# A planner's constants and twelve halved warm-up products in a two-layer attention kernel

## The chip, the core and the metric

The kernel runs on one core of a Trainium2 chip. The metric is the device time of one execution in microseconds; runs of the same kernel are given by their median and their spread. The profile is of one execution, and its times run from the first instruction.

## The reference, cut to what matters

```python
a = softmax over s of phi                      # 4 batches, 8 heads, 576 rows, 32 memory slots
k_m, v_m = a^T k, a^T v                        # 32 x 64 for each head
attn = softmax(q k_m^T / 8)                    # over the 32 slots
x = (attn @ v_m) as 2304 x 512
g = max(0.01 h, h), h = x @ w_in;   x = g @ w_out        # d_ff = 2048
g = h * tanh(softplus(h)), h = x @ w_in2; out = g @ w_out2
```

q, k, v and phi are float32; the four weight matrices arrive as float64, so the kernel has to turn each 64-bit number into a float32 by itself.

## The kernel before, in words

**Work on TensorE (PE).** Products that need float32 accuracy are made from halves: each operand is split into a rounded part (hi) and a remainder (lo), and three products hi*hi, lo*hi, hi*lo are summed. In the first layer the value matrix is folded into the weight: `vw` = v_m times a 512-wide chunk of w_in (L975), and then an item (batch, half of 288 rows, block m of 128 hidden units) is 6 products `h_t <- at_t, vw_t` (L1226) and, two items later, 12 products `acc_t <- hi_t or lo_t, wo_t` (L1259). There are 128 items. The turns are: batch 0 chunk 0 (items 0 to 7), batch 0 chunk 1 (8 to 15), batch 1 chunks 0 and 1 (from item 16), and so on. The second layer (L1579, L1791) begins near 375 us.

**The start.** Before item 0 the kernel needs batch 0's attention (phi softmax, its products L508, norm and transposes L819, q transposes L865, scores L892, softmax, then `at_t` hi and lo) and the first chunk of w_in. While PE has nothing to do it runs warm-up products: `FILL=58` products identity times identity, 128 x 128 in float32 (L1057, `spin`). They are a chain of tasks of priority 4.9, their result is not used, and the planner puts one wherever PE is idle in its plan. A float32 product of this kind stands in the trace as two records, and each record has a weight load of its own.

**Weights from float64.** `decode` takes a raw block of 128 x 512 numbers in two 32-bit words: ScalarE (ACT) scales the high word (L369), the low word is shifted right by 29 (`top`: on ACT at L374 or on VectorE, DVE, at L376), and DVE joins the two (L411). For w_out a block then gets a rounded copy (L310 on ACT or L312 on DVE) and a remainder (L326 on DVE); this is `wo_unit`. The raw blocks go round a ring of three buffers `raw` and four `raws`, in the order of the program: eight blocks of chunk 0 (four of w_in, then w_out 0 to 3), then four of w_in's chunk 1, then w_out 4 to 7.

**The order.** The program's order on every engine, and the order of the loads on the one DMA queue (SP), comes from a planner that runs while the kernel is built (`Order.run`): at each moment of its own modelled time it starts the ready task of the smallest priority number on the engine that would end it first (estimated cost plus a bias). A task that takes a buffer waits until the buffer is free. The result is fixed: each engine then runs its list in order on the chip. The constants in `K` set priorities in units of items:

- `WO`: w_out block m has the priority m - WO. `WC`: w_in's chunk c has that of its first item less WC; `V0` is the same for its product L975.
- `A1`: batch 1's attention starts that many items before item 16; `PL` and `QL` set how much earlier its loads come. `BH`: a load of batch 1 may not be issued before a certain load of w_in's chunk 1 (entry 9 means none).
- `V2`: the same as V0 for batches 2 and 3. `HFD`: the step of priority between the parts of batch 0's softmax.
- `TOP`: the bias in us against DVE when the planner chooses where `top` runs; ACT is planned at 0.61 us and DVE at 0.60 us plus `TOP`.

The planner takes a warm-up product as 0.44 us for the first 20 and 0.22 us after that, whatever its shape.

Of the kernel before, what the change touches and what calls it, by code (L numbers as in the profile page):

```python
# [23 lines left out]
def hop(a, b):  # L24
# [4 lines left out]


K = dict(
    LAG1=2, WIN=8, OB=2, RS=4, FILL=58, A1=10, S1=8.0,
    A2=30, S2=2.6, V1=2.4, V2=14, W2=45, W2S=3.8, O='phi0 kv0 phi1 q0 w0 kv1 q1 w1 w2 w3', HF0=-20.0, HF1=-7.0,
    HFD=0.3, TOP=0.1, HI=0.2, WO=2.0, WOL=1, WC=3.0, WC0=-38.0, V0=3.0, COLD=20, GL=1.5, AL=5.0, XL=22.0, T='0:1 0:1 1:2 0:2 1:2', SB=1,
    DW=280e3, DQ=1.3, DP=1.2, DS=0.78, DI=0.38, L4=0.5, L4P=1.6, L4S=0.8, L4T=5.0, MA=6, QL=4, PL=6, BH=(9,3,3,3,3), FK=-52.5, DWF=0.85, MV="......rvvrrvvrvr",
)


# [121 lines left out]
def kernel(  # L160
# [12 lines left out]
    nc = tc.nc  # L173
# [4 lines left out]
    P = 128  # L178
# [14 lines left out]
    RQ = S // 32  # L193
    LAG1 = K['LAG1']

# [75 lines left out]
    ident = const.tile([P, P], F32, name="ident")  # L271
# [11 lines left out]
    def add(engines, prio, fn, deps=(), take=(), use=(), bias=None):  # L283
        t = sched.add(engines, prio, fn, deps, take, use, bias)
        for b in (*take, *use):
            if b.pool is spool:
                early.append(t)
            elif b.pool is rawpool:
                middle.append(t)
        return t  # L290


    def dve(n):
        return n / 960 + 0.065
# [4 lines left out]
    def act(n, ps=False):  # L299
        return n / 1196 + (0.051 if ps else 0.093)  # L300

    def mm(n, count=1):
        return count * (n / 2400 + 0.0133)

    def mb(shape_bytes):
        return shape_bytes / K["DW"]

# [531 lines left out]
    def score_tasks(b, g, pq, ps, dp):  # L839
        sp = b < K['SB'] and g == 1  # L840
        if sp:
            qT, qb = qT_s.new([P, HG, NB1]), q_s.new([P, RQ, D])
            qT_v, qb_v = (lambda: qT.t), (lambda: qb.t)
        else:
            qT = qb = kvq.new([P, 2, RQ * D])
            qT_v = lambda: qb.t[:, 1].rearrange("p (h c) -> p h c", h=HG)
            qb_v = lambda: qb.t[:, 0].rearrange("p (r d) -> p r d", r=RQ)
        parts, firsts_q = [], []
        q_g = q[b, g * HG:(g + 1) * HG]

        def ld(e):
            qb.make()
            dma(out=qb_v(), in_=q_g.rearrange("h (p r) d -> (h p) r d", r=RQ))

        lq = add({"SP": K["DS"] * mb(589824)}, PQ[g], ld, (), [qb])
        for i in range(3):
            ps_b = h_tag.new([P, 3, P])

            def ftr(e, ps_b=ps_b, i=i):
                ps_b.make()  # L860
                if sp and not i:
                    qT.make()
                for j in range(3):
                    r = 2 * (3 * i + j)
                    nc.tensor.transpose(ps_b.t[:, j], qb_v()[:, r:r + 2, :].rearrange("p r d -> p (r d)"), ident)  # L865

            tt = add({"PE": 0.34}, pq + 0.7 * i, ftr, [lq, *firsts_q[:1]], [ps_b, qT] if sp and not i else [ps_b], [qb])

            firsts_q.append(tt)

            def fcp(e, i=i, ps_b=ps_b):
                copy(e, qT_v().rearrange("p h (c j) -> p j h c", j=9)[:, 3 * i:3 * i + 3], ps_b.t.rearrange("p j (h c) -> p j h c", h=HG))

            parts.append(add({"ACT": act(840, True), "DVE": dve(840)}, pq + 0.7 * i + 0.2, fcp, [tt], (), [ps_b, qT]))
        a = at_tag.new([P, 2, S], F32R)
        ab = []
        for hf in range(2):
            half(b, g, hf, ps[hf], dp, qT, qT_v, parts, a, ab)
        at[b, g] = (a, ab[0:2], ab[2:4])
# [173 lines left out]

    warm = acc_tag.slots[3].new([P, P])

    def spin(e):
        nc.tensor.matmul(out=warm.t if hasattr(warm, "t") else warm.make(), lhsT=ident, rhs=ident, start=True, stop=True)  # L1057

    last = None
    for i in range(K["FILL"]):  # L1060
        last = add({"PE": 0.44 if i < K["COLD"] else 0.22}, 4.9, spin, [last], [] if i else [warm], [warm] if i else [])
    for g in range(NG):
        kv_norm(0, g, -60.0 + 10 * g, 1.0, *kv_first(g, -60.0 + 10 * g, 1.0))
    for g in range(NG):
        score_tasks(0, g, -59.5 + 10 * g, (-54.0, K["HF0"]) if not g else (-40.0, K["HF1"]), K["HFD"])
    def next_batch(b):
        d, st = (K["A1"], K["S1"]) if b == 1 else (K["A2"], K["S2"])
        p = base[b] - d
        kv_rest(b, p, 0.08 * d / 2)
        score_rest(b, p + 0.1 * d, (p + 0.3 * d, p + 0.3 * d + st), 0.03 * d)  # L1070
# [42 lines left out]
    for n in range(NM):  # L1113
# [57 lines left out]
        def save2(e, u=u, wd=wd):  # L1171
# [13 lines left out]
                out=sb.t.rearrange("p a f -> p (a f)").bitcast(F32R), in0=sb.t.rearrange("p a f -> p (a f)"),  # L1185
# [26 lines left out]
    def passes(n):  # L1212
        return [(j, wi) for j in range(n) for wi in range(2)]

    def stage1(i, b, sub, m):
# [41 lines left out]
        def mms(todo):  # L1257
            for kk, wi, src in todo:
                nc.tensor.matmul(  # L1259
                    out=ac[kk].t,  # L1260
                    lhsT=wu[0].t[:, wi, kk * P:(kk + 1) * P],
                    rhs=(hb if src == 0 else lb).t,
                    start=(first and (wi, src) == (0, 0)),
                    stop=(last and src == 1),
                )

        hs = []
        if first:
            for kk in range(NK):
# [3 lines left out]

                hs.append(add({"PE": mm(NB1, 2)}, i + LAG1 + 0.01 * kk, f, [t4, *wu[1:], *hs[-1:]], [ac[kk]], [hb, wu[0]]))
        else:
            hs.append(
                add(
                    {"PE": mm(NB1, 2 * NK)}, i + LAG1, lambda e: mms([(kk, wi, 0) for kk, wi in passes(NK)]),
                    [t4, *wu[1:], *prev_l], (), [hb, wu[0], *ac.values()],
# [3 lines left out]
        if last:  # L1283
            for kk in range(NK):
                tl = add(
                    {"PE": mm(NB1)}, i + LAG1 + 0.1 + 0.01 * kk, lambda e, kk=kk: mms([(kk, 0, 1)]),
                    [t5, *hs], (), [lb, wu[0], ac[kk]],
# [21 lines left out]
                if add_in:  # L1309
                    deps.append(evs[kk, sub])  # L1310
                evs[kk, sub] = add(
                    {"DVE": dve(NB1)} if add_in else {"ACT": act(NB1, True), "DVE": dve(NB1)},
                    i + LAG1 + 0.2, fe, deps, [xb] if fresh else [], [ac[kk]] if fresh else [ac[kk], xb],
                )
        else:
            tl = add(
                {"PE": mm(NB1, NK)}, i + LAG1 + 0.1, lambda e: mms([(kk, 0, 1) for kk in range(NK)]),
                [t5, *hs], (), [lb, wu[0], *ac.values()],
# [577 lines left out]
```

## Time and profile before

| what | value |
|---|---|
| median of 3 runs | 742.42 us (742.01 to 742.64) |
| the profiled execution | 741.87 us |
| its span, first to last instruction | 740.1 us |
| PE busy | 731.0 us (99%) |
| DVE, ACT busy | 550.6 us (74%), 402.5 us (54%) |
| share of PE in the chain that ended last | 96% |

Some 1.8 us of the execution lie outside the span. Busy time of PE is the union of its records, whose ends are modelled; a wait shorter than that modelled tail does not show as idle time, so starts of successive records are compared as well.

### The profile page before, as it was taken

To read this page: it belongs to the slowest core of one execution; us is meant where nothing else is said; L and a number is where in the kernel's file an instruction comes from. 1 tells how busy PE (TensorE), PEld (TensorE's weight loads), DVE (VectorE), ACT (ScalarE), POOL (GpSimd) and SP (SyncE) were. 2 spreads that over 40 slices of the span, in tenths; PEclk is the share of its full clock that TensorE was granted. 3 is DMA by queue.
4 is the path that set the end of the run, shared out by engine and by line. 5 is a ranking of instruction groups with operands and counts; after the bars stand their busy time and mean duration, and the time that the engine had idled before them with its cause. 6 is when DMAs were issued, how large, how long until landed. Compare 5 with 4: busy or idle time off the path is not lost.

```text
span 740.1 us, 15587 instructions
## 1 busy us (share of the span) xinstructions
PE 731.0 (99%) x5875; PEld 701.3 (95%) x5875; DVE 550.6 (74%) x1153; ACT 402.5 (54%) x877; POOL 0.7 (0%) x6
## 2 busy tenths in 40 slices
PE   8999999999999999999999999999999999999997
PEld 7788899888999989999999999999999999999997
DVE  6899868598766965647859797867777966775595
ACT  4866458565553775645546665544464644444442
POOL 0000000000000000000000000000000000000000
PEclk9999999999999999999999999999999999999999
DMA  9793957787869587863559898788988778996475
GB/s 353 299 318 115 350 172 232 229 274 229 290 207 286 171 274 269 262 233 101 199 199 338 302 312 254 233 271 249 300 278 264 250 239 258 297 290 207 126 218 182
DMA packets 99322, 183.73 MB, mean 248 GB/s; under 512 B 8112, under 2 KB 51376, under 8 KB 99248
## 3 DMA queue, kind: packets, MB, share of 16 engines
q1 hardware_dynamic: 99248, 182.75, 75.5%
q8 instruction: 46, 0.75, 0.4%
q14 instruction: 28, 0.23, 0.1%
HBM read 140.25 MB, written 42.47 MB: 247 GB/s over the span
## 4 chain that ended last, share of the span: by engine, by line
PE 96%; DVE 2%; ACT 1%; DMA 0%; issue 0%
PE acc_t L1259 28%; PE h_t L1579 22%; PE acc_t L1791 22%; PE h_t L1226 13%; PE misc_t L1791 2%; PE misc_t L975 2%; PE acc_t L1579 2%; PE acc_t L508 1%; PE misc_t L741 1%; PE misc_t L646 1%; DMA phi_t<-in_phi_dram 0%; PE h_t L865 0%; ACT raws_t L369 0%; ACT raws_t L374 0%; PE misc_t L689 0%
## 5 line engine op out<-in xcount | busy, mean ns | idle before, releaser
L1259 PE MATMUL acc_t<-hi_t,wo_t 128*128 128x288 f32 x1024 | 160.6, 297 | 0.4 <-DVE x_t L312 0.3
L1259 PEld LDWEIGHTS acc_t<-hi_t,wo_t 128*128 128x128 f32 x1024 | 142.9, 188 | 12.2 <-issue 7.0
L1226 PE MATMUL h_t<-at_t,vw_t 128*128 128x288 f32 x768 | 123.1, 296 | 0.0
L1791 PE MATMUL acc_t<-hi_t,wo_t 128*128 128x384 f32 x448 | 114.4, 336 | 0.0
L1240 ACT ACTIVATE hi_t<-h_t 128x288 fp32r<-128x288 f32 x128 | 52.6, 411 | 111.8 <-PE acc_t L1259 105.3
L1226 PEld LDWEIGHTS h_t<-at_t,vw_t 128*128 128x128 f32 x768 | 108.5, 188 | 0.7 <-issue 0.6
L1247 DVE TENSOR_TENSOR lo_t<-e_t,hi_t 128x288 fp32r<-128x288 f32 x128 | 57.3, 450 | 47.4 <-ACT e_t L1240 21.6
L1259 PE MATMUL acc_t<-lo_t,wo_t 128*128 128x288 f32 x512 | 89.8, 297 | 0.5 <-DVE lo_t L1247 0.5
L1791 PEld LDWEIGHTS acc_t<-hi_t,wo_t 128*128 128x128 f32 x448 | 81.3, 188 | 0.0
L1259 PEld LDWEIGHTS acc_t<-lo_t,wo_t 128*128 128x128 f32 x512 | 74.7, 188 | 6.3 <-issue 5.6
L1579 PE MATMUL h_t<-xt_t,vw_t 128*128 128x384 f32 x396 | 79.4, 336 | 0.0
L1579 PE MATMUL h_t<-xt_t,wo_t 128*128 128x384 f32 x352 | 75.8, 336 | 0.0
L1791 PE MATMUL acc_t<-lo_t,wo_t 128*128 128x384 f32 x224 | 75.6, 337 | 0.0
L1758 DVE TENSOR_TENSOR lo_t<-wo_t,hi_t 128x384 fp32r<-128x384 f32 x94 | 52.0, 554 | 31.4 <-ACT hi_t L310 29.9
L1579 PEld LDWEIGHTS h_t<-xt_t,vw_t 128*128 128x128 f32 x396 | 69.3, 188 | 0.0
L310 ACT ACTIVATE hi_t<-wo_t 128x384 fp32r<-128x384 f32 x78 | 40.7, 524 | 40.7 <-PE acc_t L1791 36.4
L1579 PEld LDWEIGHTS h_t<-xt_t,wo_t 128*128 128x128 f32 x352 | 61.9, 188 | 0.0
L1240 ACT ACTIVATE e_t<-h_t 128x288 f32<-128x288 f32 x128 | 52.0, 406 | 0.0
L1791 PE MATMUL acc_t<-wo_t,hi_t 128*128 128x256 f32 x240 | 45.0, 282 | 0.0
L1604 ACT ACTIVATE wo_t<-wo_t 128x384 f32<-128x384 f32 x53 | 27.6, 522 | 30.8 <-DVE wo_t L1598 30.6
L1791 PEld LDWEIGHTS acc_t<-lo_t,wo_t 128*128 128x128 f32 x224 | 42.0, 188 | 0.0
L310 ACT ACTIVATE wo_t<-h_t 128x384 f32<-128x384 f32 x50 | 24.5, 489 | 31.1 <-PE h_t L1579 31.1
(263 smaller groups left out, 1110.0 us busy)
## 6 DMA issues: line engine op xcount, KB each, us to landing
wo_t<-tscr SPq DMA_DIRECT2D x168, 256.0 KB, 3.8
vw_t<-wsum SPq DMA_DIRECT2D x32, 512.0 KB, 4.7
win_t<-wscr SPq DMA_DIRECT2D x24, 512.0 KB, 5.5
raw_t<-in_moe_w_in_dram SPq DMA_DIRECT2D x19, 512.0 KB, 7.5
raw_t<-in_moe_w_out_dram SPq DMA_DIRECT2D x17, 512.0 KB, 5.5
wsum<-vw_t SPq DMA_DIRECT2D x16, 512.0 KB, 4.5
wo_t<-wsum SPq DMA_DIRECT2D x16, 512.0 KB, 4.3
tscr<-raw_t SPq DMA_DIRECT2D x9, 512.0 KB, 5.5
```

The source lines that it names most:

```text
L310: nc.scalar.activation(out=o, in_=i, func=AF.Copy)
L508: nc.tensor.matmul(out=acc.t[rows, :].rearrange("p (j d) -> p j d", j=2), lhsT=phv()[rows, r, :], rhs=kv.t[rows, :2304].rearrange("p (j r ...
L646: nc.tensor.matmul(out=accs_[g].t[o:o + M, :].rearrange("p (j d) -> p j d", j=2), lhsT=ph.t[rows, x, j, :], rhs=kv[g].t[rows, :, x % 2, j, :],
L975: nc.tensor.matmul(out=pss[g].t[M * (h ^ g):M * (h ^ g) + M, :], lhsT=vT[b, g][0].t[rows, g, h ^ g if b else h // 2, :], rhs=wbs[g].t[rows ...
L1226: nc.tensor.matmul(out=h.t, lhsT=us[g][0].t[:, wi, j0:j0 + P], rhs=ats[g][0].t[:, ai, cols], start=(n == 0), stop=(n == 3 * NG - 1),)
L1240: nc.scalar.activation(out=o, in_=h.t, func=AF.Prelu, alpha=0.01)
L1247: lambda e: nc.vector.tensor_tensor(out=lb.make(), in0=eb.t, in1=hb.t.bitcast(F32), op=ALU.subtract),
L1259: nc.tensor.matmul(out=ac[kk].t, lhsT=wu[0].t[:, wi, kk * P:(kk + 1) * P], rhs=(hb if src == 0 else lb).t, start=(first and (wi, src) == ( ...
L1579: nc.tensor.matmul(out=h.t, lhsT=w[:, wi, c0:c0 + P], rhs=xp[b, xi].ap()[:, j], start=(first and j == 0 and k3 == 0), stop=(j == 1 and k3 ...
L1604: lambda e: nc.scalar.activation(out=t_of[x](), in_=h.t if h else t_of[x](), func=AF.Mish),
L1758: lambda e, hb=hb, lb=lb, src=src: nc.vector.tensor_tensor(out=lb.make(), in0=src(), in1=hb.t.bitcast(F32), op=ALU.subtract),
L1791: nc.tensor.matmul(out=ac[t].t, lhsT=T[:, wi, t * P:(t + 1) * P] if wide else x.t[:, t * P:(t + 1) * P], rhs=x.t if wide else T[:, wi], st ...
```

## The change

It sets ten constants anew and adds one. `TOP` goes from 0.1 to 0.4, so the low-word shift goes to ACT unless DVE would end it 0.4 us sooner. `A1` 10 to 12 and `PL` 6 to 5 move batch 1's attention two items, and its first loads one item, ahead. `BH` lets the first q load of batch 1 go after the third block of w_in's chunk 1 and not after the fourth. `WO` 2.0 to 0.0 gives every w_out block a priority two items later. `WC` 3.0 to 3.5, `V0` 3.0 to 2.0, `V2` 14 to 13 and `HFD` 0.3 to 0.38 are smaller shifts of the same kind. `GL` is not used by the code. `CUT=12` makes each of the first twelve warm-up products two products of 64 columns, with the same 128 x 128 identity as weights; the planner's cost of the task stays.

```diff
-    LAG1=2, WIN=8, OB=2, RS=4, FILL=58, A1=10, S1=8.0,
-    A2=30, S2=2.6, V1=2.4, V2=14, W2=45, W2S=3.8, O='phi0 kv0 phi1 q0 w0 kv1 q1 w1 w2 w3', HF0=-20.0, HF1=-7.0,
-    HFD=0.3, TOP=0.1, HI=0.2, WO=2.0, WOL=1, WC=3.0, WC0=-38.0, V0=3.0, COLD=20, GL=1.5, AL=5.0, XL=22.0, T='0:1 0:1 1:2 0:2 1:2', SB=1,
-    DW=280e3, DQ=1.3, DP=1.2, DS=0.78, DI=0.38, L4=0.5, L4P=1.6, L4S=0.8, L4T=5.0, MA=6, QL=4, PL=6, BH=(9,3,3,3,3), FK=-52.5, DWF=0.85, MV="......rvvrrvvrvr",
+    CUT=12, LAG1=2, WIN=8, OB=2, RS=4, FILL=58, A1=12, S1=8.0,
+    A2=30, S2=2.6, V1=2.4, V2=13.0, W2=45, W2S=3.8, O='phi0 kv0 phi1 q0 w0 kv1 q1 w1 w2 w3', HF0=-20.0, HF1=-7.0,
+    HFD=0.38, TOP=0.4, HI=0.2, WO=0.0, WOL=1, WC=3.5, WC0=-38.0, V0=2.0, COLD=20, GL=2.5, AL=5.0, XL=22.0, T='0:1 0:1 1:2 0:2 1:2', SB=1,
+    DW=280e3, DQ=1.3, DP=1.2, DS=0.78, DI=0.38, L4=0.5, L4P=1.6, L4S=0.8, L4T=5.0, MA=6, QL=4, PL=5, BH=(9,3,3,2,3), FK=-52.5, DWF=0.85, MV="......rvvrrvvrvr",
...
+    spins = []
+
     def spin(e):
-        nc.tensor.matmul(out=warm.t if hasattr(warm, "t") else warm.make(), lhsT=ident, rhs=ident, start=True, stop=True)
+        spins.append(1)
+        o = warm.t if hasattr(warm, "t") else warm.make()
+        cuts = 2 if len(spins) <= K["CUT"] else 1
+        for x in range(cuts):
+            c = slice(x * P // cuts, (x + 1) * P // cuts)
+            nc.tensor.matmul(out=o[:, c], lhsT=ident, rhs=ident[:, c], start=True, stop=True)
```

## Rows read from the trace of the kernel before

**Rows 1.** The page's first part: busy us, share of the span, instructions.

```profile
span 740.1 us, 15587 instructions
PE 731.0 (99%) x5875; PEld 701.3 (95%) x5875; DVE 550.6 (74%) x1153; ACT 402.5 (54%) x877; POOL 0.7 (0%) x6
```

**Rows 2.** The waits of PE: engine, line, waited for, total us, times, longest.

```profile
PE h_t L865 <- issue: 1.4, 1, 1.4
...
PE acc_t L508 <- ACT phi_t L490: 0.5, 1, 0.5
PE acc_t L1259 <- DVE lo_t L1247: 0.5, 1, 0.5
PE acc_t L1259 <- DVE x_t L312: 0.3, 2, 0.2
```

**Rows 3.** Windows of the start and of the middle: PE, PEld, DVE, ACT, clock, DMA.

```profile
20.00:25.00 5.00, 3.61 (x42) 2.26 (x41) 4.18 (x13) 3.11 (x8) 0.00 (x0) 1.00 1.03 383
25.00:30.00 5.00, 5.00 (x52) 4.04 (x52) 4.69 (x14) 4.97 (x11) 0.00 (x0) 1.00 1.03 410
30.00:35.00 5.00, 5.00 (x44) 5.00 (x43) 4.87 (x12) 4.46 (x11) 0.00 (x0) 1.00 0.27 103
35.00:40.00 5.00, 4.47 (x33) 4.00 (x32) 4.93 (x13) 5.00 (x13) 0.00 (x0) 1.00 0.91 297
40.00:700.00 660.00, 659.69 (x5083) 635.60 (x5082) 490.55 (x1012) 359.81 (x793) 0.00 (x0) 1.00 0.76 247
```

**Rows 4.** Timeline of PE, start: start us, us, records, idle before and its releaser.

```profile
1.35 5.49 PE L1057 MATMUL acc_t<-ident 128*128 128x128 f32 x30 [1.35 <-POOL ident masks.py:199]
7.38 1.51 PE L508 MATMUL acc_t<-kvq_t,phi_t 32*32 32x128 f32 x48 [0.54 <-ACT phi_t L490]
...
18.30 1.51 PE L508 MATMUL acc_t<-kv_t,phi_t 32*32 32x128 f32 x48
19.74 0.44 PE L865 MATMUL h_t<-ident,qs_t 128*128 128x128 f32 x2
21.57 0.60 PE L865 MATMUL h_t<-ident,qs_t 128*128 128x128 f32 x4 [1.39 <-issue]
...
27.62 4.96 PE L1057 MATMUL acc_t<-ident 128*128 128x128 f32 x42
32.33 1.83 PE L1226 MATMUL h_t<-at_t,vw_t 128*128 128x288 f32 x12
```

**Rows 5.** Timeline of PE from 2.5 to 4.5 us, and from 5.5 to 6.5 us.

```profile
2.15 2.56 PE L1057 MATMUL acc_t<-ident 128*128 128x128 f32 x11
...
5.14 1.59 PE L1057 MATMUL acc_t<-ident 128*128 128x128 f32 x12
```

**Rows 6.** Timeline of PE from 56 to 58 us.

```profile
56.62 0.58 PE L623 MATMUL misc_t<-ones,rm_t 128*128 128x1 f32 x4
57.06 1.17 PE L1259 MATMUL acc_t<-hi_t,wo_t 128*128 128x288 f32 x7
```

**Rows 7.** The instruction queue: the whole span (page), then 19.0 to 20.4 us.

```profile
q8 instruction: 46, 0.75, 0.4%
...
q8 instruction: 1, 0.02, 4.9%
```

**Rows 8.** The low-word shift by engine, then ACT's timeline at 21.88 us.

```profile
L376 DVE TENSOR_SCALAR raw_t<-raw_t x13: 386/422/429, 17.1 to 290.1; 128x512 int32<-128x512 int32 x13
...
L374 ACT ACTIVATE raw_t<-raw_t x14: 667/688/734, 11.1 to 294.6; 128x512 int32<-128x512 uint16 x14
...
21.88 1.55 ACT L310 ACTIVATE qT_t<-h_t 128x384 f32<-128x384 f32 x2 [1.81 <-PE h_t L865]
```

**Rows 9.** Timeline of SP's queue from 26 to 35 us.

```profile
26.68 7.66 SPq L279 DMA_DIRECT2D raws_t<-in_moe_w_in_dram  x2
34.39 0.93 SPq L279 DMA_DIRECT2D kvq_t<-in_k_dram  x1
```

**Rows 10.** The products that first read batch 1's k and v (L646).

```profile
L646 PE MATMUL misc_t<-kvq_t,phi_t x432: 269/269/293, 59.6 to 219.9; 64*32 64x128 f32 x144
```

## Prediction

> **What bounds the kernel now.** I read the busy shares first. PE is busy for 731.0 of 740.1 us, DVE for 74% and ACT for 54% [rows 1], so only work on PE, or PE's waits, can move the end. The list of PE's waits comes next [rows 2]: all of them after the first instruction add up to 1.4 + 0.5 + 0.5 + 0.3 = 2.7 us. From 40 to 700 us PE is busy for 659.69 of 660 us [rows 3]. That leaves the first 40 us. There, every hole that the plan foresaw is filled with warm-up products, and these are no free cover on the chip: they stand in PE's list and run whether the next product is ready or not. The 42 records from 27.62 us end where item 0 begins, at 32.33, with no wait between [rows 4]. So the kernel's time is, nearly exactly, the sum of all PE records, warm-up included, plus 2.7 us of waits, plus a fixed tail. The 58 warm-up products are all placed in either version. An edit helps only if it takes away some of those waits, and it costs whatever PE work it adds.
>
> **The halved products.** In the plan nothing ahead of the first L508 changes: the load of phi, its softmax steps and the 15 products (30 records) in front of it keep priorities and planned costs. Twelve of the 15 become two products each, so 24 records and 24 weight loads are added ahead of 7.38 us. What does a record of 64 columns cost? No row has one. Late in the start, a record of 128 columns takes (32.33 - 27.62)/42 = 0.112 us [rows 4]. The floor is a cost by columns: two of 0.056 us for one of 0.112, nothing added. The other end is the nearest row: L623 has the same 128 x 128 float32 weights and a single column, and its four records take 57.06 - 56.62 = 0.44 us, 0.11 each [rows 6]. One column costs what 128 do, so the weight load sets the pace and 64 columns lie between two equal rows. I take 0.112: 24 x 0.112 = 2.69 us. The earliest records are slower: 11 span 2.56 us (0.23 each, the modelled tail included), 12 later span 1.59 (0.13 each) [rows 5]. That is the lower of the two clock levels, 1.2 GHz, until about 5 us, and then 2.4 GHz. The added records come after that moment, since all of it passes in either version, so they are priced at the upper level.
>
> Of the 2.69 us, 0.54 fall into the idle time ahead of L508 [rows 4], which waits for phi's exponential. L508 therefore starts 2.15 us later, near 9.5 us. From there to 20.18 PE has no other idle time, so the shift goes on undiminished.
>
> **The stall at 20.18 us.** PE stops for 1.39 us between two transposes of one group, with "issue" as the cause: nothing that the profile knows was awaited [rows 2, 4]. I read it as missing instructions. One queue carries 46 packets of 0.75 MB [rows 7]; PE and its loads have 11,750 instructions [rows 1], 255 for each packet, and one such packet is on its way between 19.0 and 20.4 us [rows 7], with the DMA engines full (share 1.03, [rows 3]). If so, the block's edge is fixed in instructions. The change puts 48 more ahead of it (24 records, 24 loads), so PE meets the edge 48 instructions sooner in the old order: five of L865 (0.44 us) and 43 of L508, whose 96 take 1.44 us (18.30 to 19.74), 0.65 us; together 1.09 us before 20.18, at 19.09 [rows 4]. With the shift PE is there at 21.24. If the block still comes at 21.57, PE waits 0.33 us, does the 1.09 us, and is at the old place at 22.66, where it used to go on at 21.57: the shift is now 1.09 us, and 1.06 of the stall has been won back. Ends: the block comes in time, and the shift is 2.15 - 1.39 = 0.76; or the whole stall stays, and it is 2.15. I take 1.1, since the DMA backlog that delays the packet hardly depends on PE.
>
> The Trainium skill, "Runtime: NRT & Kernel Launch", section "Instruction fetch mechanics", says that instructions come in blocks of 256 and that the crossing is mostly hidden. The count agrees with the 255 here; "hidden" does not agree with the 1.39 us. By that rule the stall would have another cause, and the shift would stay 2.15 us.
>
> **The order of the w_out blocks.** PE's other waits are 0.5 us for a remainder `lo_t` near 39 us and 0.3 us later [rows 2]. Between 25 and 40 us ACT and DVE are both nearly full (ACT 4.97, 4.46, 5.00; DVE 4.69, 4.87, 4.93 of 5 us, [rows 3]), and the remainder stood in line behind w_out work. With `WO` at 0 an item's evictions come ahead of later blocks, and PE itself comes 1.1 us later. Both favour a shorter wait, and a block that is now late can make a new one. Between all 0.8 us gone and none, I take 0.5 us gone. A block that is late costs more, and is a rival below.
>
> **Edits priced at nothing.** `TOP`: 23 blocks still shift on DVE (13 of them in the row shown, 0.42 us each); on ACT it is 0.69 [rows 8]. ACT has 46% idle and DVE 26%, so the move relieves the fuller engine. In the start only two can move (the first at 17.1 us), and ACT soon after idles 1.81 us for L865 [rows 8]; without that cover the join is 0.3 us later. `A1`, `PL`, `BH`: batch 1's loads. SP's queue stands from 26.68 to 34.39 because the fourth block of w_in's chunk 1 waits for a buffer that a w_out block holds; k, v and q are issued behind it [rows 9]. The third block frees the first q load (four DMAs) for the hole of 30 to 35 us, when DMA is at 0.27 [rows 3]. If w_out 0 is later, the fourth block and k and v are later too; k and v are first read at 59.6 us [rows 10], over 20 us on, which covers it. The attention steps themselves go two items ahead of w_out 4 to 7 on DVE; PE has items 8 to 15 meanwhile. `WC`, `V0`, `V2` and `HFD` move single steps by an item or less, under the same cover. If a cover fails, PE waits for the one step, 0.4 to 1.4 us.
>
> **Sum.** 2.69 - 0.54 - 1.06 - 0.5 = +0.6 us. On the profiled execution that is 741.87 + 0.6 = 742.5; that execution is 0.55 us under the median of the runs, so I state it on the median: 742.42 + 0.6 = 743.0 us. Its own range is 0.76 - 0.8 to 2.15: 742.4 to 744.6. About 0.2%, 1.5 us, is what a measurement of this kernel can tell from no change: 740.9 to 743.9 counts as the same.
>
> **The rivals.**
>
> 1. Halves cost halves (faster). If the array is paced by columns and the one-column record has a floor of its own, nothing is added, the edge of the block still moves 1.09 us ahead, and up to 1.39 + 0.8 us of waits can go: 740.2 to 742.0, most likely 741.0. Against it: one column costs as much as 128 [rows 4, 6]. It decides below about 80 ns for a record of 64 columns. 0.11.
> 2. The w_out blocks come too late (slower). A block needs scale, shift, join, rounded copy and remainder, five steps in a chain; by the two rows of the shift (0.42 and 0.69 us, [rows 8]) that is 2.1 to 3.4 us, and I take 2.9. If the plan leaves one for after item 0's evictions, PE, out of warm-up products, waits for one chain: 743.0 + 2.9 = 745.9, or 744.5 for half of it. For it: both engines are full until 40 us [rows 3]. Against it: the plan starts any ready task on an idle engine. 0.16.
> 3. The stall stays whole (the skill's rule named above, with another cause at the same place): 742.42 + 2.15 - 0.5 = 744.1. 0.12.
> 4. The clock comes up late. With half the columns in the same time, the array does less in the first 5 us. By 5.14 us some 16 records have begun ((5.14 - 1.35)/0.23); if the upper level came only with the next wide work, the other 38 of the 54 would take 0.10 us more each (0.23 less 0.13, [rows 5]): 743.0 + 3.8 = 746.8. For it: nothing in this trace runs so narrow at the lower level. Against it: once up, the clock stays at 1.00 through the 32 x 32 products of L508, after 7.38 us ([rows 3] from 20 us). 0.06.
> 5. None of it shows: the 1.1 us are absorbed by shorter waits everywhere: 742.4. 0.05.
>
> **How the numbers follow.** The forecast has 0.50, of which 0.05 lie above 743.9. Faster: 0.07 of rival 1. Slower: 0.05 + 0.13 of rival 2 + 0.07 of rival 3 + 0.06 = 0.31. Same: the rest, 0.62. For 8 in 10, the range leaves out the lower half of rival 1, the upper part of rival 2 and rival 4: 741.0 to 745.3.
>
> **What would show it.** L1057 ahead of the first L508 with 54 records; 0.11 us per record after the clock is up; L508 near 9.5 us; the idle time "issue" at a point 48 PE instructions earlier, inside the third L508 group of the second phi, and shorter than 1.39; item 0 near 33.4 us; PE's waits below 2.7 us in all. The prediction is wrong if 64-column records start 0.06 us apart, if the first L1226 is before 32.3, or if the plan spreads the warm-up products so that a new wait over 1 us stands on PE's list.

## The result and the profile after

The kernel became slower: 747.67 us median (746.28 to 747.96, six runs) against 742.13 (741.50 to 742.64, six runs) of the kernel before on the same chip, a ratio of 1.0072 [1.0061, 1.0083], or 5.5 us more. The profiled execution took 747.96 us, the longest of the six, and that of [rows 1] 741.87, so the two profiles lie 6.1 us apart.

The page of the kernel after, first part, answers to [rows 1]:

```profile
span 746.2 us, 15623 instructions
PE 738.4 (99%) x5899; PEld 708.3 (95%) x5899; DVE 553.9 (74%) x1159; ACT 400.3 (54%) x871; POOL 0.7 (0%) x6
```

PE has the 24 records that were counted on, and the span is 6.1 us longer, but PE is busy 7.4 us longer: 24 records at 0.112 us would be 2.7. The waits of PE after, which answer to [rows 2], have become shorter in all (here without the wait for the first instruction):

```profile
PE acc_t L508 <- issue: 1.2, 1, 1.2
PE acc_t L1266 <- DVE x_t L312: 0.2, 1, 0.2
```

So nothing new is waited for; the work itself got longer. The timeline of PE in the start, to be held against [rows 4] (start, length, records, idle time before; L1064, L1233 and L1266 are L1057, L1226 and L1259 of before). The row of 54 is 48 records of 64 columns and six of 128; the timeline names the shape of the first alone:

```profile
1.35 11.89 PE L1064 MATMUL acc_t<-ident 128*128 128x64 f32 x54 [1.35 <-POOL ident masks.py:199]
13.17 2.71 PE L508 MATMUL acc_t<-kvq_t,phi_t 32*32 32x128 f32 x48
15.81 0.49 PE L1064 MATMUL acc_t<-ident 128*128 128x128 f32 x2
...
16.56 1.51 PE L508 MATMUL acc_t<-kvq_t,phi_t 32*32 32x128 f32 x48
...
25.27 1.06 PE L508 MATMUL acc_t<-kv_t,phi_t 32*32 32x128 f32 x26
27.56 0.85 PE L508 MATMUL acc_t<-kv_t,phi_t 32*32 32x128 f32 x22 [1.24 <-issue]
28.34 0.87 PE L865 MATMUL h_t<-ident,qs_t 128*128 128x128 f32 x6
...
30.74 1.22 PE L892 MATMUL misc_t<-qT_t,kT_t 64*32 64x288 f32 x16
31.89 2.27 PE L1064 MATMUL acc_t<-ident 128*128 128x128 f32 x18
...
39.83 1.83 PE L1233 MATMUL h_t<-at_t,vw_t 128*128 128x288 f32 x12
```

And the record that follows the first L508 in the kernel before:

```profile
8.82 0.49 PE L1057 MATMUL acc_t<-ident 128*128 128x128 f32 x2
```

Three readings. The 54 warm-up records take 11.89 us where 30 wide ones took 5.49. The first group of L508, the same 48 products, takes 2.64 us to the next record (13.17 to 15.81) and 1.44 before (7.38 to 8.82); the second group is at the old length again. And item 0 begins at 39.83, not 32.33: 7.50 us late, more than the whole loss. The timeline of PE from 2.5 to 4.5 us and from 10 to 11 us:

```profile
2.26 2.56 PE L1064 MATMUL acc_t<-ident 128*128 128x64 f32 x11
...
9.73 1.49 PE L1064 MATMUL acc_t<-ident 128*128 128x64 f32 x6
```

Eleven records take 2.56 us early on, exactly as in [rows 5], but at 10 us the pace is still that: about 0.21 us from record to record. The six wide records ahead of L508 start 0.21 apart as well. Before, it was 0.11 from 5.3 us on. TensorE stayed at its lower level, 1.2 GHz, until the first group of L508 had run, the last of its products starting at 15.54. The records of the granted clock in the trace say so too: its rise is at 15.68 us, and at 5.31 before. (The clock column of the windows reads 1.00 ahead of the first such record, so in the start the level is read from the pace.)

The last PE record starts at 741.00 us, and at 734.88 before: 6.1 us later. So 1.4 us of the 7.5 are won back behind item 0.

### The profile page after: what moved, and what is told of

Its sections match the earlier page's. It is cut to its first block, busy times and chain, and to the rows that moved or that the text cites. A ratio compares the mean times of both kernels' runs of the same rounds, so it can differ in the third digit from the quotient of the medians.

```text
span 746.2 us, 15623 instructions
## 1 busy us (share of the span) xinstructions
PE 738.4 (99%) x5899; PEld 708.3 (95%) x5899; DVE 553.9 (74%) x1159; ACT 400.3 (54%) x871; POOL 0.7 (0%) x6
## 4 chain that ended last, share of the span: by engine, by line
PE 95%; DVE 4%; issue 1%; ACT 0%; POOLq 0%; POOL 0%; DVEq 0%
PE acc_t L1266 27%; PE h_t L1586 22%; PE acc_t L1798 21%; PE h_t L1233 13%; PE misc_t L1798 2%; PE acc_t L1586 2%; PE misc_t L975 2%; PE acc_t L1064 2%; PE acc_t L508 1%; PE misc_t L741 1%; PE misc_t L646 1%; DVE win_t L411 0%; DVE vw_t L326 0%; DVE wo_t L326 0%; PE misc_t L689 0%
## 5 line engine op out<-in xcount | busy, mean ns | idle before, releaser
L1266 PE MATMUL acc_t<-hi_t,wo_t 128*128 128x288 f32 x1024 | 160.7, 297 | 0.2 <-DVE x_t L312 0.2
L1266 PEld LDWEIGHTS acc_t<-hi_t,wo_t 128*128 128x128 f32 x1024 | 142.9, 188 | 11.6 <-issue 6.9
L1233 PE MATMUL h_t<-at_t,vw_t 128*128 128x288 f32 x768 | 122.9, 295 | 0.0
L1233 PEld LDWEIGHTS h_t<-at_t,vw_t 128*128 128x128 f32 x768 | 108.6, 188 | 0.4 <-ACT e_t L1247 0.2
L1266 PE MATMUL acc_t<-lo_t,wo_t 128*128 128x288 f32 x512 | 90.0, 297 | 0.0
L1266 PEld LDWEIGHTS acc_t<-lo_t,wo_t 128*128 128x128 f32 x512 | 74.7, 188 | 6.1 <-issue 6.1
```

What stands on the lines that cost most here:

```text
L1233: nc.tensor.matmul(out=h.t, lhsT=us[g][0].t[:, wi, j0:j0 + P], rhs=ats[g][0].t[:, ai, cols], start=(n == 0), stop=(n == 3 * NG - 1),)
L1266: nc.tensor.matmul(out=ac[kk].t, lhsT=wu[0].t[:, wi, kk * P:(kk + 1) * P], rhs=(hb if src == 0 else lb).t, start=(first and (wi, src) == ( ...
```

## The experiments

The theories, as the expectations name them: A, the narrow products hold the clock down, and that is the whole loss; B, the constants lose time as well; C, added records cost time at any width; D, which came later, an edge of PE's instruction blocks (the point where one block of its program ends and the next has to be there) that falls into the dense products of L646, 144 small ones in 2.2 us. Ratios are to the kernel before on the same chip, with 95% intervals. The expectations name runs by the labels e1 to e12 that stand in brackets here.

### The two parts alone

**The constants without the cut** (e1).

```diff
-    CUT=12, LAG1=2, WIN=8, OB=2, RS=4, FILL=58, A1=12, S1=8.0,
+    CUT=0, LAG1=2, WIN=8, OB=2, RS=4, FILL=58, A1=12, S1=8.0,
```

> The ten new constants with the warm-up products left whole. Theory A (the narrow products keep TensorE's clock at its lower level, and this is the whole loss): clock up near 5 us, item 0 near 32.3 us, and the time is that of before less the 1.4 us that the changed kernel gained after item 0: 740.7 us. Theory B (the constants lose time too, later w_out blocks above all): above 743 us. Theory C (the added records and their weight loads cost it, at any width): 740 to 742.5 us.

746.38 us, 1.0057 [1.0040, 1.0073]: the constants alone lose 4.3 us, although item 0 begins at 32.64. The waits of PE, then its timeline and the windows (PE, PEld, DVE, ACT, POOL, clock, DMA share, GB/s) around the first of them:

```profile
PE misc_t L646 <- issue: 3.1, 1, 3.1
...
PE acc_t L508 <- DMA kvq_t<-in_v_dram: 1.1, 1, 1.1
PE h_t L865 <- issue: 1.0, 1, 1.0
```

```profile
124.96 2.21 PE L646 MATMUL misc_t<-kvq_t,phi_t 64*32 64x128 f32 x141
130.27 0.41 PE L646 MATMUL misc_t<-kvq_t,phi_t 64*32 64x128 f32 x3 [3.09 <-issue]
130.61 1.98 PE L1266 MATMUL acc_t<-hi_t,wo_t 128*128 128x288 f32 x8
...
135.74 1.33 PE L1266 MATMUL acc_t<-hi_t,wo_t 128*128 128x288 f32 x8
```

```profile
125.00:130.00 5.00, 2.18 (x142) 1.93 (x142) 3.07 (x7) 1.68 (x4) 0.00 (x0) 1.00 0.93 350
130.00:135.00 5.00, 4.73 (x29) 4.26 (x36) 1.24 (x5) 1.78 (x6) 0.00 (x0) 0.66 1.14 285
```

This is a second stall of the kind of [rows 2], three records before the end of a group of 144. Behind it the granted clock averages 0.66 over five us, which costs some 1.7 us of work (0.34 x 5): eight products of L1266 take 1.98 us there and 1.33 us five us later. The kernel after has no such stall; its whole group takes 2.25 us. So the time is the one that B named, above 743 us, but not for B's reason: no w_out block is waited for.

**The cut without the constants** (e2).

```diff
+    spins = []
+
...
+        cuts = 2 if len(spins) <= 12 else 1
+        for x in range(cuts):
+            c = slice(x * P // cuts, (x + 1) * P // cuts)
+            nc.tensor.matmul(out=o[:, c], lhsT=ident, rhs=ident[:, c], start=True, stop=True)
```

> The kernel before with only its first twelve warm-up products halved. Theory A: clock up only after the last narrow record, near 13 to 16 us; L508 starts near 13.2 us, item 0 near 39.8 us, 748 to 750 us. Theory B: less than half of the loss, under 745 us. Theory C: as A in time, whatever the clock does.

750.89 us, 1.0118 [1.0100, 1.0136]: 8.8 us more, a little over A's range. Item 0 begins at 39.53, 0.3 us ahead of the kernel after, and there is a stall here too. Timeline of PE:

```profile
146.70 0.29 PE L1233 MATMUL h_t<-at_t,vw_t 128*128 128x288 f32 x1
148.53 1.28 PE L1233 MATMUL h_t<-at_t,vw_t 128*128 128x288 f32 x5 [1.53 <-issue]
149.60 1.17 PE L1266 MATMUL acc_t<-lo_t,wo_t 128*128 128x288 f32 x4
```

The parts lose 4.3 and 8.8 us, together 13.1, and yet 5.5 when both are made. Each part alone brings a stall of its own on PE's list, and the two together have neither. That is what D is about.

### Width or number

**Twelve products done twice at full width** (e3, on the kernel before).

```diff
+        for x in range(2 if len(spins) <= 12 else 1):
+            nc.tensor.matmul(out=o, lhsT=ident, rhs=ident, start=True, stop=True)
```

> The kernel before, each of the first twelve warm-up products done twice at its full 128 columns: as many records, weight loads and instructions as with the halves. Theory A: the clock is up near 5.3 us as before, the 54 records end near 9.4 us, L508 2.1 us later than before, 743 to 744.3 us. Theory C: the count of records is what costs, so the clock comes late here too, L508 near 13 us, 747 to 750 us.

**Twelve products of 64 columns, each done once** (e4, on the kernel before).

```diff
+        n = 64 if len(spins) <= 12 else P
+        nc.tensor.matmul(out=o[:, :n], lhsT=ident, rhs=ident[:, :n], start=True, stop=True)
```

> The kernel before, each of the first twelve warm-up products cut to 64 columns and done once: no record and no instruction is added, the array streams half as many columns in them. Theory A: the clock is late again; the 24 narrow records take 0.21 us each until 6.5 us and the clock comes up only after wide work, so L508 starts near 8 us and runs slowly: 743 to 747 us. Theory C: nothing is added, 742.1 us.

The first took 745.77 us, 1.0048 [1.0033, 1.0063]; the second 742.95, 1.0010 [1.0001, 1.0019]. Timelines of PE, first of the one with twice the wide products, then of the one with as many narrow ones as there were wide:

```profile
1.35 9.22 PE L1062 MATMUL acc_t<-ident 128*128 128x128 f32 x54 [1.35 <-POOL ident masks.py:199]
10.50 1.51 PE L508 MATMUL acc_t<-kvq_t,phi_t 32*32 32x128 f32 x48
...
145.47 0.92 PE L1231 MATMUL h_t<-at_t,vw_t 128*128 128x288 f32 x5 [2.34 <-issue]
```

```profile
1.35 6.77 PE L1062 MATMUL acc_t<-ident 128*128 128x64 f32 x30 [1.35 <-POOL ident masks.py:199]
8.05 2.79 PE L508 MATMUL acc_t<-kvq_t,phi_t 32*32 32x128 f32 x48
10.76 0.80 PE L1062 MATMUL acc_t<-ident 128*128 128x128 f32 x2
```

The same 54 records take 9.22 us wide and 11.89 narrow, and the L508 group behind them is fast behind the wide ones, slow behind the narrow ones. With 30 records the 24 narrow ones keep the lower level too, through L508 to 10.76; the record of the granted clock rises at 11.72. So width matters apart from number. Number matters as well: 24 wide records more delay item 0 by 3.28 us (35.61), and the same instruction count as in the cut alone brings a stall at the same L1226 product, 2.34 us. C holds for that much. Neither time was forecast: 745.77 us lies between the ranges of A and C, with the clock up at 7.51 us and the stall on top, and 742.95 just under A's.

### At the start or later

**A 32 x 32 product behind each of the wide warm-up products 21 to 32** (e5, the constants kept, no cut), meant as 48 instructions at little cost.

```diff
+        nc.tensor.matmul(out=o, lhsT=ident, rhs=ident, start=True, stop=True)
+        if 20 < len(spins) <= 32:
+            nc.tensor.matmul(out=o[:32, :32], lhsT=ident[:32, :32], rhs=ident[:32, :32], start=True, stop=True)
```

> The ten new constants, warm-up products whole, and a 32 x 32 x 32 product more behind each of the warm-up products 21 to 32 (after 22 us): 48 PE instructions more, as the halves add, for some 0.3 us. Theory D (e1 lost its time because a block of PE's instructions came late inside the 144 products of L646, and 48 instructions move that edge away): no wait of over 1 us after 40 us, clock at full level to the end, 740.5 to 741.7 us. Theory B (the constants themselves lose the 4 us): 746 us as in e1.

**The same behind products 1 to 12** (e6).

```diff
+        if len(spins) <= 12:
```

> As e5, with the twelve small products behind the first twelve warm-up products, so that PE's instructions stand exactly as in the changed kernel from the first L508 on. Theory A (width holds the clock down): clock up near 5 us, L508 within 0.6 us of 7.4 us, and the stall at the end of the third L508 group of the second phi as in the changed kernel; 740.5 to 742 us. Against it (any added record or load holds the clock): clock after 10 us, 746 us or more.

**The cut of the change, on products 21 to 32** (e7).

```diff
-        cuts = 2 if len(spins) <= K["CUT"] else 1
+        cuts = 2 if 20 < len(spins) <= 32 else 1
```

> The changed kernel with the halving moved from the warm-up products 1 to 12 to 21 to 32, where the clock is up. It prices a record of 64 columns at the upper level. By the prediction's step (the weight load sets the pace) 0.11 us each: item 0 2.7 us later than in e5, 743.2 to 744.4 us. By columns (the prediction's first rival) 0.056 us: as e5. The clock stays up in either.

They took 745.82 us, 1.0044 [1.0032, 1.0056]; 748.54 us, 1.0085 [1.0072, 1.0098]; and 743.90 us, 1.0019 [1.0010, 1.0027]. None of the three has an "issue" stall behind 40 us, as D wants of 48 instructions more. Timeline of PE with the small products late, and with the small products first:

```profile
27.29 0.49 PE L1061 MATMUL acc_t<-ident 128*128 128x128 f32 x2
27.70 0.24 PE L1063 MATMUL acc_t<-ident 32*32 32x32 f32 x2
27.88 0.49 PE L1061 MATMUL acc_t<-ident 128*128 128x128 f32 x2
```

```profile
11.02 0.80 PE L1061 MATMUL acc_t<-ident 128*128 128x128 f32 x2
11.74 0.31 PE L1063 MATMUL acc_t<-ident 32*32 32x32 f32 x2
11.98 0.80 PE L1061 MATMUL acc_t<-ident 128*128 128x128 f32 x2
...
14.53 2.10 PE L508 MATMUL acc_t<-kvq_t,phi_t 32*32 32x128 f32 x48
```

Late, a pair of a wide and a small product takes 0.59 us (27.29 to 27.88), and a wide one alone 0.22: the small one is anything but cheap, twelve cost 4.4 us, and item 0 begins at 36.94. That is why the time misses D's range and comes out where B had it, without B's stall. First, a pair takes 0.96 us, still at 11 us: the clock is low, though every warm-up product is wide. Here A as I had put it missed: it had the clock up early. That any added record holds the clock doesn't follow either, since with twice the wide products it was up at 7.51. Narrow products keep the level low, but so do wide ones that small ones break up. Whether it is the fewer columns, the greater share of weight loads or something else in such a row that counts, these runs don't tell apart.

The rise varies from run to run, but not by so much. In the ten traces that start with an unbroken row of wide products, the records of the granted clock have it at 4.40 to 7.51 us; in the four others (the change, e2, e4, e6) at 11.72 to 15.78.

The cut on later products shows its plain price. Timeline of PE, with PE already at 2.4 GHz:

```profile
24.86 4.23 PE L1064 MATMUL acc_t<-ident 128*128 128x64 f32 x36
29.03 1.09 PE L975 MATMUL acc_t<-win_t,vTb_t 64*32 64x512 f32 x16
```

These 36 records, nine halved products, all have 64 columns. From 24.86 to 29.03 they are 0.116 us each with both ends of the row, and within it they start 0.112 apart, what 128 columns cost. The time is in the range of the prediction's step. The same constants, the same cut and the same count of instructions, twenty products later, are some 3.8 us faster than the change.

### The edge of the instruction block

**The cut on products 21 to 26 only** (e9): 24 instructions, not 48.

```diff
-        cuts = 2 if len(spins) <= K["CUT"] else 1
+        cuts = 2 if 20 < len(spins) <= 26 else 1
```

> As e7 with six halved products (21 to 26) instead of twelve: 24 PE instructions more than e1, where e7 has 48. Theory D (the edge of an instruction block inside the 144 products of L646): the edge that stalled e1 lies at the 315th of that group's 320 instructions, in e7 at the 267th, here at the 291st, still near the group's end and asked for just before it began. So a stall of 2 us or more there, perhaps with the clock down behind it: 744.5 to 747 us, though the start is 1.3 us shorter than in e7. Without theory D: e7 less 1.3 us, 742.5.

747.97 us, 1.0076 [1.0062, 1.0089]: the stall is back, and the time a us above the range. Timeline of PE, and the windows:

```profile
125.12 2.04 PE L646 MATMUL misc_t<-kvq_t,phi_t 64*32 64x128 f32 x129
130.55 0.68 PE L646 MATMUL misc_t<-kvq_t,phi_t 64*32 64x128 f32 x15 [3.40 <-issue]
```

```profile
130.00:135.00 5.00, 4.45 (x41) 3.90 (x48) 1.36 (x6) 1.77 (x6) 0.00 (x0) 0.66 0.79 274
```

PE now stops after 129 of the 144 products and not after 141: 12 records and their 12 loads, the 24 instructions that were put in. The edge is fixed in instructions. The Trainium skill, "Runtime: NRT & Kernel Launch", section "Instruction fetch mechanics", says that an engine's instructions come in blocks of 256 by a DMA queue of its own; the trace agrees, since every "issue" stall named here follows PE instruction 705, 3009 or 3265 of the trace (products and weight loads, counted by their starts), and these lie multiples of 256 apart. It says also that the crossing is mostly hidden. That agrees for all but one or two of the 46 or 47 blocks of each trace, where no such stall is listed; the crossings named cost 0.4 to 3.4 us.

Why is the same edge free when it lies 48 instructions earlier? The DMA answers for 127.5 to 128.5 us, first the constants alone, then the kernel after:

```profile
q1 hardware_dynamic: 112, 0.40, 98.2%
q8 instruction: 1, 0.02, 5.8%
```

```profile
DMA packets 1, 0.02 MB, mean 16 GB/s; under 512 B 0, under 2 KB 0, under 8 KB 0
...
q8 instruction: 1, 0.02, 8.0%
```

The dense group of the kernel after:

```profile
131.73 2.25 PE L646 MATMUL misc_t<-kvq_t,phi_t 64*32 64x128 f32 x144
```

After, the block travels alone while the DMA engines rest, at 127.95, almost 4 us ahead of the dense group at 131.73 and 292 instructions ahead of its edge, and it is there before PE comes to that edge at 133.31. With the constants alone no block moves from 123.9 to 127.9 us, while q and w_out loads take 79% of the engines, and when it goes, at 127.95, PE has been standing for a us. In the traces PE goes on 2.3 to 2.7 us after the block's packet starts: 127.95 to 130.27; 128.19 to 130.55 with 24 instructions; 25.16 to 27.56 in the start of the kernel after. What differs between them is where the edge before this one lies, 256 instructions earlier: PE crosses it at 130.19 in the kernel after, ahead of the dense group, and at 125.11 and 125.12 in the two that stall, just inside it, so that some 2 us are left. No packet in any trace starts more than 294 instructions ahead of its edge, so the block seems to be asked for near the edge before. That, and how much of the delay is due to the loads, is my reading; neither was tried by itself.

**Cheaper instructions.** One run (e8) had `FILL=46` and lone small products behind 21 to 44:

```diff
-    CUT=12, LAG1=2, WIN=8, OB=2, RS=4, FILL=58, A1=12, S1=8.0,
+    CUT=12, LAG1=2, WIN=8, OB=2, RS=4, FILL=46, A1=12, S1=8.0,
...
+        if 20 < len(spins) <= 44:
```

> As e5 with FILL 46 instead of 58 and the small products behind the warm-up products 21 to 44, so that the count of PE's instructions stays that of e5. If warm-up products are plain PE time, as the prediction has it, twelve fewer take up to 2.7 us less, as far as item 0's operands are ready: the rows of before have them at about the time PE came, so 0.3 to 1.5 us under e5: 739.3 to 741. If what PE then waits for is all late, as e5.

747.48 us, 1.0086 [1.0060, 1.0112], its runs scattered from 746.94 to 761.01. 24 lone small products cost so much (item 0 at 39.39) that the run doesn't answer its question. The next (e10) put the twelve in one row behind product 20:

```diff
+        for x in range(12 if len(spins) == 20 else 0):
+            r = slice(32 * (x % 4), 32 * (x % 4) + 32)
+            nc.tensor.matmul(out=o[r, :32], lhsT=ident[r, r], rhs=ident[r, :32], start=True, stop=True)
```

> The ten new constants, warm-up products whole, and the 48 PE instructions as twelve 32 x 32 x 32 products in one row behind the warm-up product 20, four in flight at once as in L508. In e5 each of them, alone between two wide ones, cost 0.37 us; in L508's groups a record takes 0.015. So 0.6 to 1.2 us, item 0 near 33 us, no wait over 1 us after 40 us: 741 to 742.5 us.

742.18 us, 0.9998 [0.9989, 1.0007], with no stall at L646. Timeline and waits of PE:

```profile
23.91 0.39 PE L1064 MATMUL acc_t<-ident 32*32 32x32 f32 x24
```

```profile
PE h_t L1233 <- ACT e_t L1247: 1.4, 1, 1.4
```

The 48 instructions now cost 0.3 us in all (23.91 to 24.23). In the profiled execution 1.4 us were lost to a late eviction at 236 us, which the other kernels don't have; its cause stays open. The last two took eight warm-up products away, once with the constants and 20 small products in a row (e11), once on the kernel before with 8 (e12):

```diff
-    CUT=12, LAG1=2, WIN=8, OB=2, RS=4, FILL=58, A1=12, S1=8.0,
+    CUT=12, LAG1=2, WIN=8, OB=2, RS=4, FILL=50, A1=12, S1=8.0,
...
+        for x in range(20 if len(spins) == 20 else 0):
```

> As e10 with FILL 50 and 20 small products, so that the count of instructions stays. The eight warm-up products that go are those between items 0 and 4 and two before item 0. If they are plain PE time: up to 1.8 us under e10, as far as the operands are there; by the full engines of 35 to 40 us about half, so 740 to 741.5. If PE then waits for all of it: as e10.

```diff
-    LAG1=2, WIN=8, OB=2, RS=4, FILL=58, A1=10, S1=8.0,
+    LAG1=2, WIN=8, OB=2, RS=4, FILL=50, A1=10, S1=8.0,
...
+        for x in range(8 if len(spins) == 20 else 0):
```

> The kernel before with FILL 50 and eight small products behind the warm-up product 20, count of instructions unchanged. Before, PE waited 0.5 us for a remainder in this stretch although the warm-up products stood there, so the operands are the limit: gain under 0.7 us, less 0.6 for the small products: 741.5 to 742.7 us.

741.70 us, 0.9991 [0.9982, 1.0000], and 743.59 us, 1.0020 [1.0011, 1.0029], 0.2 and 0.9 us above their ranges. The new waits of PE in the former, and PE's timeline in the latter:

```profile
PE h_t L1233 <- ACT e_t L1247: 0.2, 1, 0.2
PE h_t L1233 <- DVE at_t L326: 0.2, 1, 0.2
```

```profile
39.69 0.79 PE L1266 MATMUL acc_t<-lo_t,wo_t 128*128 128x288 f32 x4 [2.18 <-DVE lo_t L1254]
```

With the constants, eight warm-up products fewer leave only short waits. Under the plan of before they turn into a wait of 2.2 us for a remainder. So the change's order does bring the operands earlier, as it would have to for the products to go; the gain that is left, at most 0.2%, can't be told from none. Still, the constants with wide warm-up products and an edge out of the way take 741.7 us where the change takes 747.7 (ratios to before of 0.9991, with eight products fewer, and 1.0072).

## Why the prediction was wrong

**The failed step.** It was "The added records come after that moment, since all of it passes in either version, so they are priced at the upper level". The moment when the clock rises was taken as a fixed time, and the runs show that it hangs on the work: behind wide products in an unbroken row it comes before L508, behind narrow ones not until L508's first group has run. Instead of 2.69 us the cut costs 6.33 up to L508 (13.17 less 7.38, and the 0.54 of idle time that it covered) and 1.20 in L508's first group, 7.5 in all. The price of 0.112 us for 64 columns was right where it belonged, at the upper level, as the later cut shows; at the lower one it is 0.21, again as for 128 columns.

**The idle time of 0.54** was covered, as the sum had it.

**The stall.** Its place was right to the instruction: of the third group 26 products run ahead of the edge, and the 22 that are left with their loads and two records of L865 with theirs are the 48. Its length was not: 1.24 us, not 0.33 (0.89 in e2, e3 and e6, which have the same 48 ahead of it). That "the DMA backlog that delays the packet hardly depends on PE" was wrong: the packet went at 25.16, 6.0 us later than before (19.21), where PE came to the group 7.0 us later, and it was 2.4 us ahead of PE's next product. Besides, the 16 products of L892 now take 1.15 us to the next record and 0.71 before, with a wait of PE's loads in their midst: 0.44 that nothing had been set aside for, and whose cause stays open. From the end of the first L508 group to item 0 the way is 0.5 us longer than before, where 1.06 was to be won.

**The order of the w_out blocks** won more than the 0.5: from item 0 to the last product 1.4 us less, of which the listed waits explain 0.6 (0.8 before, 0.2 now). The later cut won 1.3 with the same constants, so it is theirs. By starts, 0.8 of it lies in the first 8 us: from item 0 to the same product of L1226 it is 8.36 us before (32.33 to 40.69) and 7.54 after (39.83 to 47.37), and the wait for the remainder is most of that. Where the other 0.6 come from, I can't say.

**Edits priced at nothing.** In the change as made that came near, but by luck. The constants reorder PE's list, and with it what stands at the block's edge; without the 48 instructions of the cut this costs 3.1 us of stall and some 1.7 of low clock. I had followed the edge at 20 us and no other.

The terms as measured are 7.5 - 0.5 + 0.5 - 1.4 = 6.1 us, the difference of the profiled executions' last products; the medians differ by 5.5.

**The rivals.** Rival 4, with 0.06, was the case. Its 3.8 us for the start measured 3.6 (6.33 less 2.69), though the next wide work didn't raise the clock: the six wide records behind the narrow ones still ran at the lower level. Its 746.8 us lack the slow group of L508: 746.8 + 1.2 = 748.0, near the measured 747.7. That it comes so near is partly luck, since 1.6 us more were lost at the stall and L892 and 0.9 more won behind item 0 than its sum had. What I held against it, that the clock stays up through L508's small products, concerns a clock that is up already, and says nothing of raising it. Rival 1 fell (64 columns cost as much as 128), rival 2 left no sign (no wait for a w_out block), rivals 3 and 5 don't fit a start that is 7.5 us longer.

## What to carry to other kernels

In this kernel the warm-up work raises the clock, so it should be wide and unbroken until the pace of the records shows that the clock is up; narrowing it, or putting small products between, costs twice, in itself and in the real work behind it. An instruction more or less early in an engine's list moves every later edge of its instruction blocks, so a change of a few instructions can bring or take a stall of 3 us a hundred us later, and parts of a change measured alone don't add up; look first where long "issue" waits stand. Where the DMA engines are busy and a dense run of small instructions takes up the stretch between two edges, the second edge can be dear; a dozen 32 x 32 products in one row move it for 0.3 us.

## What the runs showed of the hardware beside this

- A lone 32 x 32 product between two 128 x 128 ones costs 0.37 us (0.59 for the pair, 0.22 for the wide one); twelve in a row cost 0.3 us together.
- The clock's rise is not fixed even with the same wide start: the 30 first records took from 5.06 us (small products late) to 6.47 us (cut on 21 to 26), where the kernel before had 5.49.
- A pause of PE may be followed by the lower clock, and need not be: after pauses of 3.1, 3.4 and 1.5 us the granted clock fell (0.66, 0.66 and, from 145 to 155 us of the cut alone, 0.89 and 0.77), after one of 2.3 us, with the products done twice, and one of 2.2 us, in the last run, it didn't.
- The same load of v came in time for the first L508 in some runs and 0.3 to 1.7 us late in others, with the same constants: L508 starts at 7.23 us with the cut on later products, without that wait, and at 8.08 with the small products late, after 1.7 us of it.
